# Attention units split into three steps in a fused attention and mixture kernel on one Trainium2 core

## Chip, core and metric

The kernel runs on one core of a Trainium2 chip. The metric is the device time of one execution in microseconds, as the median of several runs; lower is better. The profile is of one more execution of the same program. Its engines are PE (matrix products; its weight loads are shown as PEld), DVE, ACT and POOL (elementwise work), and SP, which issues the DMA transfers.

## What is computed

Three stages follow each other, all in float32.

```
scores = q @ k.T / sqrt(64), masked to 32 keys (heads 0-3) or 32 keys with stride 4 (heads 4-7)
x      = softmax(scores) @ v                      # 4 batches, 8 heads, 576 positions -> 2304 x 512
g      = sigmoid(x @ w_gate) * (x @ w_val)        # 512 -> 1536
x      = g @ w_out                                # 1536 -> 512
logits = x @ phi                                  # 2304 x 32 slots
slots  = softmax over tokens(logits).T @ x        # 32 x 512
slots  = relu(slots @ w1[e]) @ w2[e]              # 8 experts, 4 slots each
out    = softmax over slots(logits) @ slots
```

## The kernel before

The 2304 tokens are five blocks: blocks 0 to 3 have 512 tokens each, block 4 has 256. The attention of a block is four units, each a pair of heads. A unit goes through scores (a group of products of 32 by 64 at line 170 that fills two PSUM banks `s_ps`), a softmax (largest value at L184 and difference at L187 on DVE, exponential at L196 on ACT, sum and reciprocal at L201 to L203 on DVE, division at L207 on POOL), a turn of the probabilities (`turn_unit`, transposes at L219, a copy by ACT at L220 into `pt_ring`), the weighted sums of values (`weighted`, products of 64 by 32 at L246), and `finish_unit`, which takes the sums out of PSUM into the operand `x_hi`, `x_lo` of the next stage. The sums of unit z-2 are written into the free halves of the two banks that unit z's scores use.

The gated layer of a block is twelve tiles. A tile is two halves, a = 0 for the gate and a = 1 for the value; a half is twelve products of 128 by 512 at L494 into one of two PSUM banks `l1ps`. A tanh on ACT (L505) empties the first, a multiplication on DVE (L480) the second; the product of the next tile that uses the bank has to wait for it. The weights of a tile are split into a high and a low part (`whl`, L451 on ACT and L452 on DVE or POOL), in two buffers.

In the head (`first_block`) the four units of block 0 are worked off in an order written by hand, with the first products of tile 0 between them. There `fixed[0]` is true and the instructions keep the order of the program on each engine. After that a scheduler places them, but for the attention's instructions on PE and the loads, which stay in order among themselves. While the twelve tiles of block 0 run, their weights come from packed integers: a transfer into `st`, a top part by ACT (L380), a shift and a low part on DVE (L384, L387), two sums on POOL (L391), and a transfer back to memory. This is `convert`, and `ahead(z)` calls it for tile z. In the same loop the units of blocks 1 to 4 are interleaved: `attn_steps` makes a list of steps, and a `Spread` object, called once after each half, emits as many of them as its table of marks (count of halves, steps due) asks for.

The steps of before are two kinds. `sp_step(z)` has the scores of unit z, at once behind them the weighted sums of unit z-2, the softmax of z, the finish of z-2 and loads; `t_step(z-1)` turns unit z-1. While the tiles of block 1 run, six further conversions give the matrix w_out, and `slot_weights` has each go through four small steps, due some halves later by the list `later`: two turns (`wt_ps`, L428), one product with phi (`pt_ps`, L434), and one sum of products (`wp_ps`, L443). From there on the kernel has no attention: blocks 2 and 3 run their layer with a seven-product scheme (`pa`, `pd`, `pe` at L618), block 4 and the slots' sums follow, then the experts and the output.

Of the kernel before, what the change touches and what calls it, by code (L numbers as in the profile page):

```python
# [22 lines left out]
NF = 12  # L23
# [30 lines left out]
def tile_kernel(  # L54
# [154 lines left out]
    def softmax(u, norm):  # L209
        soft_max(u)  # L210
        soft_exp(u)
        soft_sum(u)
        soft_norm(u, norm)
# [87 lines left out]
    def attn_steps(pbs, norm):  # L301
        jobs = [(n, hp) for n in pbs for hp in HP_ORDER]
        us = [{"id": j, "z": z} for z, j in enumerate(jobs)]

        def load_qk(z):
            if z < len(us):
                start_unit(us[z], "qk")

        def load_v(z):
            if z < len(us):  # L310
                start_values(us, z)

        begun = []

        def first(what):
            if what not in begun:
                begun.append(what)
                what(0)
                what(1)

        def sp_step(z):
            if z < len(jobs):
                if z == 0:
                    first(load_qk)
                    first(load_v)
                scores(us[z], range(4))
                if 2 <= z:
                    weighted(us[z - 2], range(2), us[z])
                softmax(us[z], norm)
                load_qk(z + 2)  # L330
                if z == 0:
                    load_v(2)
            if z >= 2:
                if z >= len(jobs):
                    weighted(us[z - 2], range(2))
                finish_unit(us[z - 2])
                load_v(z + 1)

        def t_step(z):
            turn_unit(us[z])  # L340

        steps = []
        for z in range(len(jobs) + 2):
            steps += [(sp_step, z)] + ([(t_step, z - 1)] if 0 < z <= len(jobs) else [])
        return steps, lambda: first(load_qk), lambda: first(load_v)


# [63 lines left out]
    ticks = [0]  # L411
    later = []
# [7 lines left out]
    def slot_weights(f, wo_f, lag):  # L420

        wt = pm.rearrange("p a b -> p (a b)").rearrange("p (k c x) -> p k c x", k=ND, c=2)
        at_ = {}

        def turned(c):
            wt_ps = ps_a.tile([P, ND, P], F32, tag="a", name="wt_ps")
            for kc in range(ND):
                nc.tensor.transpose(wt_ps[:, kc], wo_f[:, c, P * kc : P * kc + P], ident)  # L428
            nc.scalar.copy(wt[:, :, c], wt_ps)

        def product():
            pt_ps = ps_m.tile([P, 2, P], F32, tag="m", name="pt_ps")
            for kc in range(ND):
                nc.tensor.matmul(  # L434
                    pt_ps[32 * kc : 32 * kc + 32], lhsT=phi[:, kc, :], rhs=wt[:, kc], start=True, stop=True
                )
            at_["pt"] = acc[:, 2, 0:256].rearrange("p (c x) -> p c x", c=2)
            nc.vector.tensor_copy(at_["pt"], pt_ps)

        def summed():  # L440
            wp_ps = ps_m.tile([P, 2, 32], F32, tag="m", name="wp_ps")
            for c in range(2):
                nc.tensor.matmul(wp_ps[:, c], lhsT=at_["pt"][:, c], rhs=i4, start=True, stop=True)  # L443
            nc.vector.tensor_scalar(wp[:, f : f + 2], wp_ps, 0.5, None, ALU.mult)

        for n, (step, *args) in enumerate(((turned, 0), (turned, 1), (product,), (summed,))):
            later.append((ticks[0] + lag + n, step, args))

    def split_half(whl, src, h, eng):
        src = src.rearrange("p (a k c) -> p a k c", a=2, k=ND)  # L450
# [6 lines left out]
    def split_w(src, pool=(True, False)):  # L457
        whl = new_w()
        for h in range(2):
            split_half(whl, src, h, nc.gpsimd if pool[h] else nc.vector)  # L460
        return whl
# [407 lines left out]
    conv = {}  # L869

    def ahead(z):
        if z < NF:
            conv[z] = convert(z)
# [21 lines left out]
    def first_block():  # L895
# [43 lines left out]
        whl = new_w()  # L939
# [7 lines left out]
        convert_end(0, fw[0])  # L947
        fw[1] = convert_begin(1)
        first_qk()
        first_v()  # L950
        g = l1_tile(0, 0)
        pt = [ps_l1.tile([P, 512], F32, tag="l1", name="l1ps") for _ in range(2)]

        def chunk(dc):
            for a in range(2):
                l1_chunk(0, whl, a, pt[a], dc)
# [11 lines left out]
        whl1 = new_w()  # L968
# [3 lines left out]
        split_half(whl1, fw[1][:, 1], 1, nc.vector)  # L972
        convert_end(1, fw[1])
        ahead(2)
        chunk(HP_ORDER[2])
        chunk(HP_ORDER[3])
        for a in range(2):
            l1_gate(g, a, pt[a])
        return whl1

    steps, first_qk, first_v = attn_steps([1, 2, 3, 4], nc.gpsimd)
    sab = Spread(steps, [(2, 0), (2 * NF - 2, 10), (4 * NF - 4, len(steps))])
    fixed[0] = True
    whl = first_block()
    fixed[0] = False
    ahead(3)
    sab.n = 2

    def load_w(z):
# [2 lines left out]
            ld(nc.sync.dma_start(wst[z], wg32[z]))  # L992

    for f in range(1, NF):
        whl = split_w(conv.pop(f), (False, False)) if f > 1 else whl
        ahead(f + LA + 1)
        if f >= 10:
            store()
            load_w(f - 10)
        l1(0, f, whl, sab)  # L1000
        if f == 3:
            pad_stream()
# [44 lines left out]
    for f in range(NF):  # L1047
        whl = split_w(wst[f // 2][:, f % 2])
# [436 lines left out]
```

## Time and profile before

| what | us |
|---|---|
| median of 3 runs | 482.8 |
| lowest, highest run | 481.75, 483.62 |
| the profiled execution | 484.0 |
| its span, first to last instruction | 482.2 |
| outside the span | 1.8 |
| PE busy, share of the span | 465.4, 97% |
| DVE, ACT, POOL busy | 302.9, 211.7, 159.0 |

A page of the profile gives the busy time of each engine, then groups of instructions by line. In a timeline each row has its start and its length in microseconds, the engine, the line, the operation, what is written and read, and how many equal ones follow each other. Square brackets at the end hold the idle time of the engine just ahead of the row and the line that released it; "issue" stands for a wait for nothing that the profile shows. The length of a matrix product contains the time in which it drains, while the next is under way already, so the pace of PE is the distance between starts and not the length.

### The profile page before, as it was taken

How to read it: one execution, taken by the hardware profiler on the slowest of the kernel's cores; microseconds unless marked ns; L12 is line 12 of the kernel's file. 1: busy time of each engine (PE TensorE's matmuls, PEld its weight loads, DVE VectorE, ACT ScalarE, POOL GpSimd, SP SyncE). 2: the span in 40 equal slices, each digit the busy share in tenths (PEclk: the TensorE clock that was granted, in tenths of full speed). 3: DMA queues.
4: the chain of work that ended last, by engine and by line, in shares of the span. 5: the costliest groups of instructions: out<-in, count | busy, mean ns of one | idle time of the engine just before them, and what ended most of it. 6: DMA issues, size and time to landing. Idle time of an engine off the chain costs nothing.

```text
span 482.2 us, 12644 instructions
## 1 busy us (share of the span) xinstructions
PE 465.4 (97%) x5424; PEld 357.8 (74%) x5424; DVE 302.9 (63%) x591; ACT 211.7 (44%) x395; POOL 159.0 (33%) x134
## 2 busy tenths in 40 slices
PE   7899999999989999999999999999999999999993
PEld 3577788887868787686788888888887889842552
DVE  5867899666567675467776566656547765532623
ACT  2645555435445544444355545554535344300222
POOL 1335566226444843612033332333312124110100
PEclk9999999999989999999999999999999999999998
DMA  8997999775995883022220220210599986589966
GB/s 327 416 390 255 395 331 370 258 266 193 344 386 215 271 307 121 37 90 87 90 87 1 88 88 1 87 54 34 176 374 419 349 335 236 217 330 368 427 242 239
DMA packets 23720, 112.12 MB, mean 233 GB/s; under 512 B 2288, under 2 KB 7152, under 8 KB 14576
## 3 DMA queue, kind: packets, MB, share of 16 engines
q1 hardware_dynamic: 23664, 111.32, 61.6%
q8 instruction: 42, 0.69, 0.5%
q14 instruction: 14, 0.11, 0.1%
HBM read 97.16 MB, written 14.16 MB: 231 GB/s over the span
## 4 chain that ended last, share of the span: by engine, by line
PE 87%; DVE 5%; POOL 2%; ACT 2%; issue 2%; DVEq 0%; POOLq 0%; ACTq 0%
PE l1ps L494 32%; PE pa L618 13%; PE pe L618 7%; PE tp L751 4%; PE so_ps L1314 3%; PE pd L618 3%; PE s_ps L246 3%; PE h_ps L1252 3%; PE s_ps L170 3%; PE sp L776 2%; PE lt_ps L722 2%; POOL fw L391 2%; PE wt_ps L428 1%; PE tr L219 1%; PE op L1352 1%
## 5 line engine op out<-in xcount | busy, mean ns | idle before, releaser
L494 PE MATMUL l1ps<-x_hi,whl 128*128 128x512 f32 x384 | 130.9, 405 | 0.9 <-ACT g L505 0.9
L494 PEld LDWEIGHTS l1ps<-x_hi,whl 128*128 128x128 f32 x384 | 72.8, 190 | 17.4 <-ACT g L505 1.8
L494 PE MATMUL l1ps<-x_lo,whl 128*128 128x512 f32 x192 | 75.8, 395 | 0.0
L391 POOL TENSOR_TENSOR fw<-fw 128x512 int32<-128x512 int32 x36 | 48.5, 1366 | 43.9 <-DVE fw L384 23.7
L494 PEld LDWEIGHTS l1ps<-x_lo,whl 128*128 128x128 f32 x192 | 36.6, 191 | 6.7 <-DVE x_lo L275 0.4
L480 DVE SCALAR_TENSOR_TENSOR g<-g,l1ps 128x512 f32<-128x512 f32 (+1 forms) x36 | 21.4, 595 | 27.0 <-PE l1ps L494 26.8
L494 PE MATMUL l1ps<-x,whl 128*128 128x256 f32 x288 | 37.0, 285 | 0.0
L494 PEld LDWEIGHTS l1ps<-x,whl 128*128 128x128 f32 x288 | 35.4, 192 | 0.4 <-ACT whl L451 0.2
L505 ACT ACTIVATE g<-l1ps 128x512 f32<-128x512 f32 (+1 forms) x36 | 18.9, 524 | 35.7 <-PE l1ps L494 35.5
L452 POOL TENSOR_TENSOR whl<-w,whl 128x512 fp32r<-128x512 f32 x12 | 15.9, 1326 | 51.3 <-ACT whl L451 39.7
L452 POOL TENSOR_TENSOR whl<-wst,whl 128x512 fp32r<-128x512 f32 x12 | 15.9, 1323 | 33.8 <-ACT whl L451 28.8
L452 DVE TENSOR_TENSOR whl<-fw,whl 128x512 fp32r<-128x512 f32 x24 | 23.7, 1001 | 5.2 <-ACT whl L451 4.7
L207 POOL TENSOR_TENSOR sm<-sm,su 128x512 f32<-128x512 f32 x14 | 18.9, 1353 | 22.0 <-DVE su L203 22.0
L751 PEld LDWEIGHTS tp<-cst,g 128*128 128x128 f32 x192 | 21.3, 140 | 5.4 <-issue 4.1
L751 PE MATMUL tp<-cst,g 128*128 128x128 f32 x192 | 25.0, 275 | 0.0
L756 ACT COPY gt<-tp 128x512 f32<-128x512 f32 x24 | 14.0, 584 | 24.1 <-PE tp L751 21.4
L184 DVE TENSOR_REDUCE mx<-s_ps 128x4 f32<-128x256 f32 x40 | 15.1, 415 | 14.4 <-PE s_ps L246 9.5
L681 DVE TENSOR_TENSOR tm<-pe,tm 128x512 f32<-128x512 f32 x12 | 8.3, 692 | 24.6 <-PE pe L618 24.6
L380 ACT ACTIVATE fw<-st 128x1024 f32<-128x1024 f32 x18 | 20.7, 1149 | 4.9 <-DMA st<-wd 4.9
L451 ACT CAST whl<-fw 128x512 fp32r<-128x512 f32 x24 | 14.6, 624 | 15.4 <-POOL fw L391 9.1
L451 ACT CAST whl<-wst 128x512 fp32r<-128x512 f32 x24 | 14.3, 618 | 15.1 <-PE l1ps L494 10.7
L246 PE MATMUL s_ps<-pt_ring,v 64*64 64x32 f32 (+1 forms) x992 | 17.9, 220 | 2.4 <-issue 1.6
(485 smaller groups left out, 958.1 us busy)
## 6 DMA issues: line engine op xcount, KB each, us to landing
ew<-w SPq DMA_DIRECT2D x32, 1024.0 KB, 7.8
st<-wd SPq DMA_DIRECT2D x18, 1024.0 KB, 8.7
wst<-wg SPq DMA_DIRECT2D x12, 1024.0 KB, 5.8
v<-qkv SPq DMA_DIRECT2D x20, 512.0 KB, 7.0
wg<-fw SPq DMA_DIRECT2D x12, 512.0 KB, 5.5
w<-wg SPq DMA_DIRECT2D x6, 1024.0 KB, 6.7
qk<-qkv SPq DMA_DIRECT2D x10, 576.0 KB, 6.0
qk<-qkv SPq DMA_DIRECT2D x8, 528.0 KB, 5.5
```

The source lines that it names most:

```text
L184: kp(nc.vector.tensor_reduce(mx[:, 4 * r : 4 * r + 4], u["s_ps"][r], AX.X, ALU.max))
L207: kp(norm.tensor_tensor(s, s, u["su"].unsqueeze(2).to_broadcast([P, 8, 64]), ALU.mult))
L246: nc.tensor.matmul(o, lhsT=v[k, t, i, r, :], rhs=p_[k, 2 * r + t, i, 0:nq], start=True, stop=True)
L380: return kp(nc.scalar.activation(fw[:, 0, c], staged[z][:, c, 1].bitcast(F32), AF.Prelu, scale=2.0**-112, alpha=2.0**32))
L391: kp(nc.gpsimd.tensor_tensor(low, top, low, ALU.add))
L451: kp(nc.scalar.copy(whl[:, 0, h], src[:, h]))
L452: kp(eng.tensor_tensor(whl[:, 1, h], src[:, h], whl[:, 0, h].bitcast(F32), ALU.subtract))
L480: return nc.vector.scalar_tensor_tensor(g, g, 1.0, val, ALU.add, ALU.mult)
L494: nc.tensor.matmul(pt, lhsT=whl[:, w_, a, dc, :], rhs=x_[n][:, dc, :], start=(dc == HP_ORDER[0] and (w_, x_) == (0, x_hi)), stop=(dc == HP ...
L505: return nc.scalar.activation(g, pt, AF.Tanh, scale=0.5) if a == 0 else gated(g, pt)
L618: nc.tensor.matmul(pt, lhsT=w[:, w_, P * c : P * c + P], rhs=x_[:, c], start=first and c == 0 and w_ == 0 and x_ is hi, stop=c == 1 and w_ ...
L751: nc.tensor.transpose(tp[:, c], g_sb[self.n, 4 * q + c][:, P * j : P * j + P], ident)
```

## The change

The step of a unit's scores (`s_step`) no longer holds the weighted sums of the unit two before. These, with their finish and the load of values, are a step of their own (`w_step`), placed behind the turn of the unit between. For the four units of block 4 the sums stay inside the step of the scores. The marks of `Spread` are new: from 10 steps at the end of block 0's tiles to 16 (of a list that has 44 steps and not 34), with a mark for the start. In the head the loads of values for the first units of block 1 are issued behind the conversion of tile 2, and the conversion of tile 3 and the split of tile 2's weights are called before the head's end, so that they keep the program's order. The last of the four small steps of `slot_weights` is due one half later (n + n // 3 gives 0, 1, 2, 4).

```
-        def sp_step(z):
-            if z < len(jobs):
-                if z == 0:
-                    first(load_qk)
-                    first(load_v)
-                scores(us[z], range(4))
-                if 2 <= z:
-                    weighted(us[z - 2], range(2), us[z])
-                softmax(us[z], norm)
-                load_qk(z + 2)
-                if z == 0:
-                    load_v(2)
-            if z >= 2:
-                if z >= len(jobs):
-                    weighted(us[z - 2], range(2))
-                finish_unit(us[z - 2])
-                load_v(z + 1)
+        def s_step(z):
+            if z == 0:
+                first(load_qk)
+                first(load_v)
+            scores(us[z], range(4))
+            if us[z]["id"][0] == 4:
+                w_step(z - 2)
+            softmax(us[z], norm)
+            load_qk(z + 2)
+            if z == 0:
+                load_v(2)
...
+        def w_step(z):
+            weighted(us[z], range(2), us[z + 2] if z + 2 < len(jobs) else None)
+            finish_unit(us[z])
+            load_v(z + 3)
...
         for z in range(len(jobs) + 2):
-            steps += [(sp_step, z)] + ([(t_step, z - 1)] if 0 < z <= len(jobs) else [])
+            if z < len(jobs):
+                steps.append((s_step, z))
+            if 0 < z <= len(jobs):
+                steps.append((t_step, z - 1))
+            if z >= 2 and (z >= len(jobs) or jobs[z][0] < 4):
+                steps.append((w_step, z - 2))
...
-            later.append((ticks[0] + lag + n, step, args))
+            later.append((ticks[0] + lag + n + n // 3, step, args))
...
         first_qk()
-        first_v()
         g = l1_tile(0, 0)
...
         ahead(2)
+        first_v()
         chunk(HP_ORDER[2])
         chunk(HP_ORDER[3])
         for a in range(2):
             l1_gate(g, a, pt[a])
-        return whl1
+        ahead(3)
+        return whl1, split_w(conv.pop(2), (False, False))
...
-    sab = Spread(steps, [(2, 0), (2 * NF - 2, 10), (4 * NF - 4, len(steps))])
+    sab = Spread(steps, [(2, 0), (5, 1.5), (2 * NF - 2, 16), (4 * NF - 4, len(steps))])
...
-    ahead(3)
...
-        whl = split_w(conv.pop(f), (False, False)) if f > 1 else whl
+        whl = split_w(conv.pop(f), (False, False)) if f > 2 else begun[f - 1]
```

From line 318 on the lines of the changed kernel stand up to four further down: L380 is L384 there, L451 is L455, L494 is L498, L505 is L509.

The first place is ACT at the end of the head, from the conversion of tile 2 on. Before:

```order
L380 ACTIVATE fw<-st 128x1024
L505 ACTIVATE g<-l1ps 128x512
L451 CAST whl<-fw 128x512 x2
L196 ACTIVATE sm_96<-sm_96 128x512
L380 ACTIVATE fw<-st 128x1024
L505 ACTIVATE g<-l1ps 128x512
```

And now:

```order
L384 ACTIVATE fw<-st 128x1024
L509 ACTIVATE g<-l1ps 128x512
L384 ACTIVATE fw<-st 128x1024
L509 ACTIVATE g<-l1ps 128x512
L455 CAST whl<-fw 128x512 x4
L196 ACTIVATE sm_96<-sm_96 128x512
```

The tanh of tile 1 (the second `g<-l1ps`) stood behind the exponential of block 1's first unit (L196) and tile 3's conversion (L380); it now stands ahead of the exponential.

The second place is PE in block 1's tiles, at the unit whose scores are in `s_ps_2016` and `s_ps_2017`; the rows of scores (L170) and of sums (L246) repeat, 32 of each, and the first of each bank stands for them. Before:

```order
L156 MATMUL s_ps_2017<-msk 128x256
L170 MATMUL s_ps_2016<-qk 32x64
L170 MATMUL s_ps_2017<-qk 32x64
...
L246 MATMUL s_ps_2016<-pt_ring,v_1682 64x32
L246 MATMUL s_ps_2017<-pt_ring,v_1682 64x32
...
L434 MATMUL pt_ps<-pm,cst 32x256 x4
L428 MATMUL wt_ps<-cst,fw 128x128 x4
```

And now:

```order
L156 MATMUL s_ps_2017<-msk 128x256
L170 MATMUL s_ps_2016<-qk 32x64
...
L438 MATMUL pt_ps<-pm,cst 32x256 x4
L432 MATMUL wt_ps<-cst,fw 128x128 x4
L498 MATMUL l1ps<-x_hi,whl 128x512
...
L219 MATMUL tr<-cst,sm_96 128x128 x4
L432 MATMUL wt_ps<-cst,fw 128x128 x4
L498 MATMUL l1ps<-x_hi,whl 128x512
...
L246 MATMUL s_ps_2016<-pt_ring,v_1702 64x32
```

The weighted sums that followed the scores at once now come behind two halves of a tile (two groups of twelve L498) and the turn of another unit.

The third place is POOL at the end of block 1's tiles, where `pt_ring<-pt_ring,su` is the division of a unit's softmax, the last such row being the last unit's. Before:

```order
L546 TENSOR_TENSOR tsum<-xf 128x512 x2
L452 TENSOR_TENSOR whl<-wst,whl 128x512
L207 TENSOR_TENSOR pt_ring<-pt_ring,su 128x512
L546 TENSOR_TENSOR tsum<-xf,tsum 128x512 x4
L452 TENSOR_TENSOR whl<-wst,whl 128x512 x2
```

And now:

```order
L207 TENSOR_TENSOR pt_ring<-pt_ring,su 128x512
L550 TENSOR_TENSOR tsum<-xf,tsum 128x512 x2
L456 TENSOR_TENSOR whl<-wst,whl 128x512
L207 TENSOR_TENSOR pt_ring<-pt_ring,su 128x512
L550 TENSOR_TENSOR tsum<-xf,tsum 128x512 x2
L456 TENSOR_TENSOR whl<-wst,whl 128x512
```

The last unit's division now stands behind one more split of weights, that of the last tile; the split before it (tile 10) is among rows further up.

## Rows read from the trace of the kernel before

**Rows 1.** The page: busy time by engine, instruction transfers, a group of lines.

```profile
PE 465.4 (97%) x5424; PEld 357.8 (74%) x5424; DVE 302.9 (63%) x591; ACT 211.7 (44%) x395; POOL 159.0 (33%) x134
q8 instruction: 42, 0.69, 0.5%
```

**Rows 2.** Stretches: length, then busy time (instructions) by engine, granted clock, DMA.

```profile
40.00:130.00 90.00, 90.00 (x1446) 72.67 (x1444) 68.65 (x121) 44.94 (x76) 46.15 (x34) 1.00 0.85 308
130.00:210.00 80.00, 77.82 (x1235) 61.53 (x1232) 51.59 (x107) 40.32 (x78) 39.50 (x31) 0.98 0.61 214
```

**Rows 3.** PE's waits: line, who released it, total, times, longest.

```profile
PE s_ps L246 <- issue: 1.6, 1, 1.6
...
PE wp_ps L443 <- DVE x L275: 0.6, 1, 0.6
```

**Rows 4.** Timeline, SP, ACT and PE at the end of the head.

```profile
20.91 0.91 SPq L299 DMA_DIRECT2D v<-qkv  x2
22.95 0.33 SPq L360 DMA_DIRECT2D st<-wd  x1
...
35.58 0.63 ACT L196 ACTIVATE sm<-sm 128x512 f32<-128x512 f32 x1 [2.08 <-DVE sm L187]
36.12 1.11 ACT L380 ACTIVATE fw<-st 128x1024 f32<-128x1024 f32 x1
...
36.48 0.39 PE L494 MATMUL l1ps<-x_hi,whl 128*128 128x512 f32 x1
...
37.12 0.59 ACT L505 ACTIVATE g<-l1ps 128x512 f32<-128x512 f32 x1
...
37.76 0.50 PE L494 MATMUL l1ps<-x_hi,whl 128*128 128x512 f32 x1 [0.89 <-ACT g L505]
```

**Rows 5.** Timeline, PE at the unit of 137 us.

```profile
137.24 0.86 PE L170 MATMUL s_ps<-qk 64*32 64x64 f32 x64
...
138.03 0.82 PE L246 MATMUL s_ps<-pt_ring,v 64*64 64x32 f32 x41
...
140.41 0.55 PE L246 MATMUL s_ps<-pt_ring,v 64*64 64x32 f32 x23 [1.56 <-issue]
```

**Rows 6.** The stretch behind it, columns as in rows 2.

```profile
140.00:146.00 6.00, 5.59 (x46) 4.37 (x47) 3.44 (x9) 1.90 (x4) 0.00 (x0) 0.72 1.02 419
```

**Rows 7.** Timeline, PE: sums that stand alone between two halves.

```profile
205.04 1.12 PE L246 MATMUL xp<-pt_ring,v 64*64 64x16 f32 x64
206.09 0.50 PE L494 MATMUL l1ps<-x_hi,whl 128*128 128x512 f32 x1
206.43 0.39 PE L494 MATMUL l1ps<-x_lo,whl 128*128 128x512 f32 x1
206.66 0.62 PE L494 MATMUL l1ps<-x_hi,whl 128*128 128x512 f32 x2
```

**Rows 8.** Timeline, PE, ACT and POOL from the last unit's scores to its turn.

```profile
186.99 0.39 PE L156 MATMUL s_ps<-msk 128*128 128x256 bf16 x2
...
189.16 0.63 PE L443 MATMUL wp_ps<-cst,acc 128*128 128x32 f32 x4
189.62 0.64 PE L428 MATMUL wt_ps<-cst,fw 128*128 128x128 f32 x4
...
192.88 0.60 PE L219 MATMUL tr<-cst,pt_ring 128*128 128x128 f32 x4
193.19 1.04 POOL L207 TENSOR_TENSOR pt_ring<-pt_ring,su 128x512 f32<-128x512 f32 x1 [3.97 <-DVE su L203]
...
193.97 0.50 PE L494 MATMUL l1ps<-x_hi,whl 128*128 128x512 f32 x1
...
196.92 0.67 PE L246 MATMUL xp<-pt_ring,v 64*64 64x32 f32 x32
197.07 1.14 ACT L451 CAST whl<-wst 128x512 fp32r<-128x512 f32 x2 [2.92 <-POOL tsum L546]
...
199.17 1.73 POOL L452 TENSOR_TENSOR whl<-wst,whl 128x512 fp32r<-128x512 f32 x1
```

More of the change, by code (lines that the diff above doesn't have):

```diff
@@ L978, in first_block @@
             l1_gate(g, a, pt[a])
-        return whl1
+        ahead(3)
+        return whl1, split_w(conv.pop(2), (False, False))
     steps, first_qk, first_v = attn_steps([1, 2, 3, 4], nc.gpsimd)
-    sab = Spread(steps, [(2, 0), (2 * NF - 2, 10), (4 * NF - 4, len(steps))])
+    sab = Spread(steps, [(2, 0), (5, 1.5), (2 * NF - 2, 16), (4 * NF - 4, len(steps))])
     fixed[0] = True
-    whl = first_block()
+    begun = first_block()
     fixed[0] = False
-    ahead(3)
     sab.n = 2
```

## The prediction

> **What bounds the kernel now.** I read the busy table first: PE is busy for 465.4 of 482.2 us, 97% [rows 1], and the next engine for 302.9. So PE's own order decides, and a change can only give back time in which PE stands still or runs slowly, or cost such time. Then the stretches in which the change works: from 40 to 130 us PE has no gap at all, and from 130 to 210 us it is busy for 77.82 of 80 us at a granted clock of 0.98 [rows 2]. Then PE's waits, of which three lie in the part that is reordered: 1.6 us inside the weighted sums with no releaser that the profile shows, 0.6 us for DVE ahead of a sum of products [rows 3], and 0.89 us for a tanh at the end of the head [rows 4]. Behind 210 us the instructions of PE stand in the same order as before, so what lies there only shifts.
>
> All that can be won is therefore small: these three waits, and what the clock loses behind the first of them.
>
> **The change part by part.** The sum is made against the profiled execution, 484.0 us (a span of 482.2 and 1.8 around it). It is 1.2 us above the median of 482.8, so it may hold more of a stall that comes and goes than a usual run does.
>
> *The head.* PE's product of tile 2 waits from the end of the half that starts its last product at 36.48 until 37.76 [rows 4]. Products follow each other at 0.23 us (206.43 to 206.66 in [rows 7]), so 1.28 - 0.23 = 1.05 us are lost. It waits for the tanh that starts at 37.12, and that stood on ACT behind the exponential (35.58, held for 2.08 us by DVE) and tile 3's conversion (36.12). In the new order of ACT the tanh stands ahead of the exponential, and only the conversion precedes it. That needs its transfer: the load of `st` is issued at 22.95, once its buffer is free, with two loads of values just ahead of it (20.91) that now stand behind. Its data can only come earlier. Even a conversion that starts as late as 33 us, with 1.11 us, lets the tanh end at about 34.7, well ahead of 36.7. So 1.05 us go. The two loads of values are first read by the first weighted sums of block 1, which stand behind the scores of two more units, so I cost their delay at nothing; the split of tile 2's weights, now in fixed order, also keeps its place ahead of PE, though with little to spare. Bounds: 1.05 won, or nothing.
>
> *Scores and sums apart.* At 138 us PE gets through 41 of 64 products of the sums, stands still for 1.56 us and goes on [rows 5]; nothing that the profile shows releases it. The scores have 64 products and 64 weight loads, the sums as many. The page has 42 instruction transfers of 0.69 MB together, against 5424 products and 5424 loads on PE [rows 1]: 10848 / 42 = 258 instructions for each. On the mean such a load lasts 482.2 / 42 = 11.5 us, but scores and sums in one piece use one up in 2.17 us (186.99 to 189.16 in [rows 8]). I therefore take the stall for a lack of instructions, in a piece that uses them five times as fast as the mean. The change breaks these pieces: of 14 units whose scores are followed at once by sums, the four of block 4 remain, and one place has sums and then scores. At the place of the stall two halves of a tile lie between. I count the 1.56 us as gone. Behind the stall the clock is granted at 0.72 over 6 us [rows 6], which is time at 1.2 GHz and not 2.4; PE has just stood still and then only had small products. It cost 6 x 0.28 = 1.7 us, which goes too. Together 3.3 us; bounds 0 and 3.3.
>
> The Trainium skill (Runtime: NRT & Kernel Launch, section Instruction fetch mechanics) says that the sequencer fetches the next block while it executes the current one, so that crossing a block is mostly hidden. By that rule the stall is none of instructions, breaking the pieces wins nothing, and the sum is higher by 3.3 us; that is the second rival below. The row with its 1.56 us and no releaser speaks against it here, without settling it.
>
> *More breaks.* Every group of small products between two halves has its price: the first product behind it takes 0.34 us to the next start (206.09 to 206.43) where others take 0.23 [rows 7]. Sums alone take 1.05 us (205.04 to 206.09), about what they add behind scores, so the group itself costs nothing more. In the new order of PE 42 groups stand between halves where 36 stood, so 6 x 0.11 = 0.7 us are added. Bounds: 0.3 and 1.2.
>
> *Later sums of products.* The wait of 0.62 us for DVE at 200 us [rows 3] came from a sum of products that needed a PSUM buffer of the last units' sums. Half a tile later the buffer should be free: 0.6 us won, at worst nothing. The other five such sums had no wait, so their delay brings nothing.
>
> *The last unit's turn.* Here a wait is added. The last unit's scores come one half later than before, with one half and eight products left until its turn. From their start to the turn PE has scores and sums 2.17 us, the turn of another unit and a product with phi 1.09 (192.88 to 193.97), a sum of products 0.46 (189.16 to 189.62), a half of 2.95 (193.97 to 196.92) and eight products of 0.23 with one break, 1.95: in all 8.6 us [rows 8]. The division that this turn needs now stands on POOL behind a split of tile 11's weights, and the cast that the split needs starts when the half has ended (197.07 against 196.92), which is 2.17 + 0.46 + 1.09 + 2.95 = 6.7 us from the scores. Then one cast of two in 1.14 us, 0.57; POOL's split of 1.73; the division of 1.04: 10.0 us. PE waits about 1.4 us, and what is queued behind the turn on PE, four products and the last sums, waits with it. Bounds: 0, if the scheduler's order gives way, and 2.0, if POOL waits for both casts.
>
> *Banks.* A unit's two banks are now held until its later sums, half a tile longer, and the transposes `wt_ps` share the four banks. Each unit still ends its use ahead of the next but one's scores, so I take nothing.
>
> The sum: 484.0 - 1.05 - 3.3 - 0.6 + 0.7 + 1.4 = 481.15, so 481.1 us. Against the median of 482.8 that is 0.35% less, inside the 0.5% (2.4 us) that a measurement of this kernel can tell from no change; faster begins below 480.4, slower above 485.2.
>
> **The rivals.** *The last turn does not wait.* If the division is done in time, 1.4 us are saved: 479.7 us, faster. For it: POOL stood idle for 3.97 us ahead of the same division before [rows 8]. Against it: the order of POOL.
>
> *The change does not remove the stall.* If what holds PE at 138 us is not the density of instructions, the stall and its clock come back somewhere in the run: 481.1 + 3.3 = 484.4 us, no change. For it: the other thirteen dense pieces had no such wait; against it: this one lies in the middle of one, at a time when DMA, which brings the instructions too, is busy throughout (1.02 in [rows 6]).
>
> *The clock falls in a longer lump.* In two places at the end of block 1, turn, scores, sums, sum of products, product with phi and transposes now stand in one row, 2.17 + 1.09 + 0.46 = 3.7 us and the transposes, without a product of a tile [rows 8]. If the clock goes down behind one as in [rows 6], 1.7 us: 482.8 us, no change.
>
> *The tanh falls behind in block 0's tiles.* This one ends slower. In the new order of ACT a tanh still stands behind an exponential at four later tiles, and exponentials wait for DVE, whose queue now gets a unit's scores earlier and more of them before tile 12 (16 steps against 10). Where the exponential, a conversion and the tanh start only when the bank is wanted, PE waits 0.63 + 1.11 + 0.59 = 2.3 us [rows 4]; at half of that in four places 4.6 us: 485.7 us. It decides from the point where the exponential starts later than a half's 12 x 0.23 = 2.75 us behind its tanh's product. Against it: from 40 to 130 us PE had no gap at all with similar queues [rows 2].
>
> **How the numbers follow.** Forecast, 481.1 us: 0.45, of which 0.06 lie below 480.4. Last turn without a wait, 479.7: 0.22. Stall remains, 484.4: 0.15. Clock in a lump, 482.8: 0.06. Tanh behind, 485.7: 0.12. Faster by over 0.5%: 0.22 + 0.06 = 0.28. Slower: 0.12. Within: 0.60. The range goes from 479.3, the first rival with the low end of the breaks, to 484.6, just over the stall that remains; it leaves out the slower rival and a little below, some 0.18. Most of the chance lies on one side of zero or within, so it needs no second range.
>
> **What would show it.** Right: no wait of PE at the end of the head; none inside scores or sums, and a clock of 1.00 from 130 to 210 us; one wait of 1 to 2 us of the last turn for POOL near 200 us; PE's first product of block 0's logits 2 to 4 us earlier. Wrong: an idle time "issue" inside sums again; waits of products for the tanh between 50 and 110 us; a stretch at half clock; waits of the scores for a bank or a load.

## The result, and the profile after

The changed kernel takes 485.83 us in the median of 13 runs (483.51 to 488.75), the kernel before 482.8 (13 runs, 481.12 to 484.29); the ratio is 1.0065, with a 95% interval of 1.004 to 1.0091. It is 0.65% slower, and 485.83 lies outside the range of 479.3 to 484.6. The prediction was wrong. All ratios compare fast runs; of the experiment f3 the profiled execution (491.94 us) was a slow one, and only the places and lengths of single stalls are read from it.

The page of the profiled execution (488.5 us), two lines that answer to [rows 1], and the stretches of [rows 2], with the two in which the clock fell (length, busy time and instructions by engine, granted clock, DMA share, GB/s):

```profile
PE 469.4 (96%) x5424; PEld 358.0 (74%) x5424; DVE 305.3 (63%) x591; ACT 212.0 (44%) x395; POOL 158.6 (33%) x134
q8 instruction: 42, 0.69, 0.5%
```

```profile
40.00:130.00 90.00, 89.79 (x1381) 71.03 (x1380) 67.92 (x126) 43.78 (x75) 42.10 (x32) 1.00 0.81 289
130.00:210.00 80.00, 76.56 (x1245) 60.18 (x1244) 51.45 (x103) 39.54 (x76) 41.67 (x33) 0.98 0.61 223
170.00:178.00 8.00, 7.09 (x119) 5.63 (x102) 3.53 (x12) 1.49 (x3) 2.89 (x4) 0.79 0.49 117
...
425.00:435.00 10.00, 9.94 (x63) 4.78 (x62) 3.42 (x8) 0.93 (x3) 0.98 (x1) 0.83 0.72 275
```

From 130 to 210 us PE is busy for 1.3 us less than before, so it stands still more, and the clock still falls there, 30 us later than in [rows 6]. PE's waits, against [rows 3]:

```profile
PE tr L219 <- POOL pt_ring L207: 1.8, 1, 1.8
PE s_ps L246 <- issue: 1.6, 2, 0.9
...
PE l1ps L498 <- ACT g L509: 0.2, 1, 0.2
```

The wait of `wp_ps` for DVE is gone, and that for the tanh at the end of the head (the 0.2 us that are left for a tanh lie at 58.7 us and cost 0.3 from start to start): on ACT the conversion stands ahead and the tanh behind it starts 4 us earlier than in [rows 4].

```profile
30.86 1.14 ACT L384 ACTIVATE fw<-st 128x1024 f32<-128x1024 f32 x1 [0.87 <-DMA st<-wd]
33.09 0.60 ACT L509 ACTIVATE g<-l1ps 128x512 f32<-128x512 f32 x1 [1.10 <-PE l1ps L498]
```

The idle time "issue" inside the sums has the same total of 1.6 us, now in two places. The wait of the last turn for POOL is new. PE's timeline (start, time busy, idle before) at the two stalls, against [rows 5]:

```profile
163.33 0.90 PE L246 MATMUL s_ps<-pt_ring,v 64*64 64x32 f32 x46
164.92 0.53 PE L246 MATMUL s_ps<-pt_ring,v 64*64 64x32 f32 x18 [0.69 <-issue]
...
170.19 0.55 PE L246 MATMUL s_ps<-pt_ring,v 64*64 64x32 f32 x22
171.65 0.83 PE L246 MATMUL s_ps<-pt_ring,v 64*64 64x32 f32 x42 [0.91 <-issue]
```

Both units are of block 4, the ones whose sums the change leaves behind their scores. From start to start the two stalls cost 0.91 and 1.13 us, the one of before 1.78. What follows at half clock costs 8 x 0.21 = 1.7 us, as in [rows 6], and a spell between 425 and 435 us another 1.7, where the order of PE is that of before.

The turn of the last unit, on PE, DVE and POOL, against [rows 8]:

```profile
198.53 0.69 DVE L484 SCALAR_TENSOR_TENSOR g<-g,l1ps 128x512 f32<-128x512 f32 x1 [0.80 <-PE l1ps L498]
199.14 0.20 DVE L203 RECIPROCAL su<-su 128x8 f32<-128x8 f32 x1
```

```profile
199.36 1.28 POOL L456 TENSOR_TENSOR whl<-wst,whl 128x512 fp32r<-128x512 f32 x1 [5.12 <-ACT whl L455]
200.60 1.49 POOL L207 TENSOR_TENSOR pt_ring<-pt_ring,su 128x512 f32<-128x512 f32 x1
```

```profile
199.92 0.39 PE L498 MATMUL l1ps<-x_lo,whl 128*128 128x512 f32 x1
202.15 0.66 PE L219 MATMUL tr<-cst,pt_ring 128*128 128x128 f32 x4 [1.83 <-POOL pt_ring L207]
```

The wait is there for the reason given: POOL's split stands ahead of the division. On DVE the gate of a half, which cannot start before that half ends, also stands ahead of the reciprocal (198.53 ahead of 199.14), but it does not count here: the reciprocal is done at 199.34, and POOL is busy with the split until 200.6. Start to start the wait costs 2.23 - 0.23 = 2.0 us. From the start of the unit's scores (191.69) PE comes to the turn in 8.5 us, and POOL is done with the division after 10.4: the cast ahead of the split starts 0.3 us later than in the forecast, and the split 0.1 us later behind it.

The breaks, a half that ends in scores (first four rows) and one that ends in sums standing alone, against [rows 7]:

```profile
61.36 0.39 PE L498 MATMUL l1ps<-x_hi,whl 128*128 128x512 f32 x1
61.59 0.39 PE L156 MATMUL s_ps<-msk 128*128 128x256 bf16 x2
...
62.70 0.50 PE L498 MATMUL l1ps<-x_hi,whl 128*128 128x512 f32 x1
63.03 0.40 PE L498 MATMUL l1ps<-x_lo,whl 128*128 128x512 f32 x1
...
68.54 0.39 PE L498 MATMUL l1ps<-x_hi,whl 128*128 128x512 f32 x1
68.85 1.14 PE L246 MATMUL s_ps<-pt_ring,v 64*64 64x32 f32 x64
69.92 0.50 PE L498 MATMUL l1ps<-x_hi,whl 128*128 128x512 f32 x1
70.26 0.39 PE L498 MATMUL l1ps<-x_lo,whl 128*128 128x512 f32 x1
```

Into the scores a product takes its usual 0.23 us (61.36 to 61.59), into the sums 0.31 (68.54 to 68.85); out of either 0.33 to 0.34. So sums alone add 70.26 - 68.54 - 2 x 0.23 = 1.26 us to the tile where sums behind scores add 1.06 (the experiment h4 below shows such a piece): 0.20 more. Ten units have their sums apart now, 2.0 us. The whole stretch agrees: from the first product of tile 2 to the first product of the logits, with waits and half clock taken out, PE needs 167.1 us before and 169.0 after.

The profiled executions then add up: head -1.05, `wp_ps` -0.8, stalls +0.26 (2.04 for 1.78), clock behind them 0, breaks +2.0, last turn +2.0, the tanh at 58.7 us +0.3, the spell at 425 us +1.7: +4.4 of the 4.5 us between 484.0 and 488.5.

### The profile page after: what moved, and what is told of

It reads as the page before. It is cut to its first block, busy times and chain, and to the rows that moved or that the text cites. A ratio compares the mean times of both kernels' runs of the same rounds, so it can differ in the third digit from the quotient of the medians.

```text
span 486.7 us, 12643 instructions
## 1 busy us (share of the span) xinstructions
PE 469.4 (96%) x5424; PEld 358.0 (74%) x5424; DVE 305.3 (63%) x591; ACT 212.0 (44%) x395; POOL 158.6 (33%) x134
## 4 chain that ended last, share of the span: by engine, by line
PE 89%; DVE 6%; issue 2%; ACT 1%; POOL 1%; ACTq 0%; DVEq 0%; POOLq 0%
PE l1ps L498 31%; PE pa L622 13%; PE pe L622 6%; PE tp L755 4%; PE s_ps L246 3%; PE so_ps L1318 3%; PE pd L622 3%; PE h_ps L1256 3%; PE s_ps L170 3%; PE sp L780 2%; PE lt_ps L726 2%; PE tr L219 2%; DVE whl L456 2%; PE wt_ps L432 1%; PE idle L116 1%
## 5 line engine op out<-in xcount | busy, mean ns | idle before, releaser
L498 PE MATMUL l1ps<-x_hi,whl 128*128 128x512 f32 x384 | 131.9, 406 | 0.2 <-ACT g L509 0.2
L498 PEld LDWEIGHTS l1ps<-x_hi,whl 128*128 128x128 f32 x384 | 72.6, 190 | 16.9 <-ACT g L509 0.7
L498 PE MATMUL l1ps<-x_lo,whl 128*128 128x512 f32 x192 | 75.8, 395 | 0.0
L395 POOL TENSOR_TENSOR fw<-fw 128x512 int32<-128x512 int32 x36 | 49.7, 1402 | 43.9 <-DVE fw L388 30.0
L498 PEld LDWEIGHTS l1ps<-x_lo,whl 128*128 128x128 f32 x192 | 36.5, 190 | 6.5 <-DVE x_lo L275 0.4
L498 PE MATMUL l1ps<-x,whl 128*128 128x256 f32 x288 | 37.0, 285 | 0.0
L498 PEld LDWEIGHTS l1ps<-x,whl 128*128 128x128 f32 x288 | 35.4, 192 | 0.4 <-ACT whl L455 0.2
L509 ACT ACTIVATE g<-l1ps 128x512 f32<-128x512 f32 (+1 forms) x36 | 18.9, 524 | 27.4 <-PE l1ps L498 27.2
L207 POOL TENSOR_TENSOR sm<-sm,su 128x512 f32<-128x512 f32 x14 | 16.3, 1162 | 35.1 <-DVE su L203 34.7
L456 DVE TENSOR_TENSOR whl<-fw,whl 128x512 fp32r<-128x512 f32 x24 | 22.7, 964 | 3.9 <-ACT whl L455 3.5
L196 ACT ACTIVATE sm<-sm 128x512 f32<-128x512 f32 x16 | 10.1, 632 | 29.2 <-DVE sm L187 29.2
L384 ACT ACTIVATE fw<-st 128x1024 f32<-128x1024 f32 x18 | 20.7, 1152 | 4.3 <-DMA st<-wd 4.3
L455 ACT CAST whl<-wst 128x512 fp32r<-128x512 f32 x24 | 14.0, 622 | 19.1 <-PE l1ps L498 11.4
L455 ACT CAST whl<-fw 128x512 fp32r<-128x512 f32 x24 | 14.5, 621 | 16.5 <-POOL fw L395 9.9
```

The costliest lines, as they stand in the source:

```text
L207: kp(norm.tensor_tensor(s, s, u["su"].unsqueeze(2).to_broadcast([P, 8, 64]), ALU.mult))
L384: return kp(nc.scalar.activation(fw[:, 0, c], staged[z][:, c, 1].bitcast(F32), AF.Prelu, scale=2.0**-112, alpha=2.0**32))
L395: kp(nc.gpsimd.tensor_tensor(low, top, low, ALU.add))
L455: kp(nc.scalar.copy(whl[:, 0, h], src[:, h]))
L456: kp(eng.tensor_tensor(whl[:, 1, h], src[:, h], whl[:, 0, h].bitcast(F32), ALU.subtract))
L498: nc.tensor.matmul(pt, lhsT=whl[:, w_, a, dc, :], rhs=x_[n][:, dc, :], start=(dc == HP_ORDER[0] and (w_, x_) == (0, x_hi)), stop=(dc == HP ...
```

## The experiments

### What each part does

First each part alone on the kernel before. *e1_head*: the head's hunks of the change.

```
-        first_v()                        # from ahead of l1_tile
+        first_v()                        # to behind ahead(2)
...
+        ahead(3)
+        return whl1, split_w(conv.pop(2), (False, False))
```

> The kernel before with the change in the head alone (tile 3's conversion and tile 2's split ordered in the head, the loads of values later); the order of PE stays. If the head is worth what the trace of after shows there (the wait of the last product of tile 2 gone, 1.05 us), the time is 1.0 us under before (ratio 0.9978) and the chip's profile shows no wait of an l1ps product for a tanh near 37 us. The rival, that the time won is lost again in a stall of instructions further on, since everything behind runs an us earlier against the loads: 0 to +2 us, with an idle time called issue in scores or sums.

481.31 us against 481.45; ratio 0.9995 (0.9969 to 1.0022). The wait of the head is gone from the trace, and the stall stays where it was. The interval holds both -1.05 us (0.9978) and nothing: the time alone does not show the gain.

*e2_steps*: `s_step`, `t_step`, `w_step` and the new spread.

```
-        def sp_step(z):
+        def s_step(z): ...   def w_step(z): ...
-    sab = Spread(steps, [(2, 0), (2 * NF - 2, 10), (4 * NF - 4, len(steps))])
+    sab = Spread(steps, [(2, 0), (5, 1.5), (2 * NF - 2, 16), (4 * NF - 4, len(steps))])
```

> The kernel before with the steps apart and their new spread alone (head and sums of products as before). From the two traces: breaks of the rows of products cost 2.2 us more than before, the last unit's turn waits 1.8 to 2.0 us for POOL, and a stall of instructions with its clock costs as much as it did before or less. Theory one, the steps are the whole loss: 482.8 + 2.2 + 2.0 = 487.0 us (ratio 1.0085), or 484 us where the stall is gone too. Rival, the loss comes from the three parts together (buffers shared by the later sums of products): within 1 us of before.

487.51 us; ratio 1.0105 (1.0065 to 1.0145): the loss is in the steps, by its middle value more than in the whole change, though the two intervals overlap. Besides the breaks and the wait of the last turn (1.8 us again), a turn at 52 us waits, since without the head's new order the softmax of block 1's first unit comes late:

```profile
51.86 0.39 PE L498 MATMUL l1ps<-x_hi,whl 128*128 128x512 f32 x1
53.98 0.66 PE L219 MATMUL tr<-cst,sm 128*128 128x128 f32 x4 [1.73 <-POOL sm L207]
```

So the new spread needs the new head. And the wait of `wp_ps` for DVE is gone here without the later sums of products.

*e3_later*:

```
-            later.append((ticks[0] + lag + n, step, args))
+            later.append((ticks[0] + lag + n + n // 3, step, args))
```

> The kernel before with the sums of products half a tile later alone. If the wait of wp_ps for DVE (0.6 us near 200 us) goes and nothing else moves: 482.2 us, ratio 0.9988. Rival: the wait is taken over by the next user of the bank, ratio 1.000, with a wait of PE of 0.5 us or more for DVE or ACT near 200 us.

484.27 us; ratio 1.0051 (1.0024 to 1.0077), slower, which neither theory had. The wait of `wp_ps` goes, but 40 us earlier the later sum now stands just ahead of a product with phi, and the copy of `wp_ps` (162.45 on DVE) stands behind a conversion's shift and a step of a softmax (161.31, 1.23 us). The product starts 0.15 us after the copy is done (162.66); the brackets name the reciprocal that ends just behind it, at 162.77, when PE's wait is already over:

```profile
161.02 0.63 PE L428 MATMUL wt_ps<-cst,fw 128*128 128x128 f32 x4
...
162.45 0.21 DVE L444 TENSOR_SCALAR wp<-wp_ps 128x64 f32<-128x64 f32 x1
...
162.81 0.64 PE L434 MATMUL pt_ps<-pm,cst 128*32 128x256 f32 x8 [1.16 <-DVE su L203]
```

And a second stall in sums appears at 167.9 us (0.92 us), at 36 of 64.

*e4_head_later*: both edits.

> The kernel before with the head and the later sums of products, without the steps apart. If the parts add up: -1.05 - 0.6 = -1.65 us, 481.1 us, ratio 0.9966, the fastest of all so far. If the stall in the sums at 138 us depends only on where the blocks of instructions end, which these two edits leave as it was there, it stays at 1 to 1.6 us; if it depends on what the DMA does at the time, it may go or come elsewhere, 1.5 to 3.3 us to either side.

483.01 us; ratio 1.0024 (0.9992 to 1.0055). The same two stalls (0.73 and 0.89) and the same wait of the product for DVE, 1.2: what the head gives, the later sums take.

### The last turn and the breaks

*f1_last_dve*, on the changed kernel:

```
-            softmax(us[z], norm)
+            softmax(us[z], norm if z + 1 < len(jobs) else nc.vector)
```

> The changed kernel with the last unit's division on DVE instead of POOL, nothing else. If the wait of 1.8 us ahead of the last turn is the division behind the weight split on POOL, it goes and the time is 1.8 to 2.0 us under that of the changed kernel: 483.9 us or a ratio of 1.0025 to before. Rival: DVE's own queue (the gate of the half, the splits) holds the division as long, or what it displaces on DVE (a low part of weights) makes the next half wait: a wait of 1 us or more ahead of the turn or of an l1ps product stays, ratio 1.005 or more.

483.57 us against 482.55; ratio 1.001 (0.9988 to 1.0033), 0.55% under the changed kernel's. The wait shrinks, but does not go:

```profile
196.31 0.39 PE L498 MATMUL l1ps<-x_lo,whl 128*128 128x512 f32 x1
197.73 0.63 PE L219 MATMUL tr<-cst,pt_ring 128*128 128x128 f32 x4 [1.03 <-DVE pt_ring L207]
```

Without POOL's split 0.8 us are won. Now the gate ahead of the reciprocal does count, since the division follows it on the same engine, and the division takes 1.82 us on DVE (195.75). The profiled execution also had only one stall, of 0.40 us, so not all of the 0.55% need be the last turn's.

*f2_sums_behind*, on the changed kernel:

```
-            if us[z]["id"][0] == 4:
+            if z >= 2:
                 w_step(z - 2)
...
-                steps.append((w_step, z - 2))
+                steps.append((w_step, z - 2) if z >= len(jobs) else (none,))
```

> The changed kernel with every unit's sums directly behind the scores of the next but one again, as in block 4; the spread, the head and the later sums of products stay as changed. 38 rows of products of a tile instead of 43, and no sums that stand alone but the last. If a break costs 0.11 us, as the prediction had it, 0.55 us come back; if going from a product of a tile into the sums costs 0.21 us, where going into scores costs 0.13, and a turn ahead of sums 0.53 instead of 0.35, as the trace of after shows, 1.5 to 2.2 us come back. Against both: more pieces of 130 products and loads, so a stall of instructions of 1 us or more may show in one that had none.

486.03 us; ratio 1.0073 (1.0039 to 1.0107), no gain in time. In the trace the stretch from the first product of tile 2 to the first product of the logits, with waits and half clock taken out, is 167.1 us instead of 169.0 in the changed kernel: 1.9 us less, which is what 0.2 us for each unit's sums gives, and not 0.55. In this execution a stall of 2.7 us at 138 us, back in the piece that is whole again, its spell of half clock and a turn's wait of 0.9 us stand against the gain.

### What the stall is

PE's instructions can be counted in the trace: products, weight loads and the few that wait for a semaphore. In thirteen profiled executions of ten kernels 20 stalls of over 0.2 us lie inside sums between 40 and 215 us. Every one comes when the count is 193 or 194 past a multiple of 256 (by products and loads alone it would be 162 to 177), and every one ends 1.25 to 1.51 us after an instruction transfer has landed. The Trainium skill (Runtime: NRT & Kernel Launch, Instruction fetch mechanics) has instructions refilled in blocks of 256, which agrees. A block below is what one such transfer brings.

*f3_after_pad0* and *g1_head_pad4* shift the counts: eight or four fewer padding products, each of which stands in the trace as two products and two loads.

```
-PAD = 8
+PAD = 0        # on the changed kernel
...
-PAD = 8
+PAD = 4        # on the kernel before with the changed head
```

> The changed kernel without the 8 padding products of 128x8 that stand near 51 us (they cost 0.24 us together). Every instruction of PE behind them moves 32 places against the ends of the blocks in which instructions are loaded. If the stalls at 164 and 170.5 us are late blocks, asked for at 157.6 and 163.8 us while all DMA engines are full, they go, since the block ends then fall near 146, 155 and 166 us and not ahead of a dense piece; with them their clock, 2.0 + 1.7 us: 482 us, ratio 0.999. Rival: the stalls belong to these pieces themselves (a bank, a value that the profile does not name): they stay where they are and the time falls by 0.24 us alone, ratio 1.006.

> The kernel before with the changed head, and 4 padding products instead of 8 (0.12 us less; every instruction of PE behind 51 us moves 16 places against the block ends). If the stall of 1.5 us in the sums at 137 us is a late block, it goes (the block ends fall near 124, 135 and 147 us) and the time is 1.05 + 1.5 + 0.12 us under before, with the clock up to 1.7 more: 478.8 us, ratio 0.9944 or lower. Rival: the stall stays at its place, or comes back in a piece where a block end now falls: ratio 0.997 to 1.000.

485.15 us, ratio 1.0059 (1.0034 to 1.0083), and 482.54 us, ratio 0.9997 (0.9969 to 1.0024): the stalls did not go. But they moved inside their pieces, of f3:

```profile
167.65 1.13 PE L246 MATMUL s_ps<-pt_ring,v 64*64 64x32 f32 x62
169.13 0.30 PE L246 MATMUL s_ps<-pt_ring,v 64*64 64x32 f32 x2 [0.35 <-issue]
...
174.16 0.78 PE L246 MATMUL s_ps<-pt_ring,v 64*64 64x32 f32 x38
177.05 0.59 PE L246 MATMUL s_ps<-pt_ring,v 64*64 64x32 f32 x26 [2.11 <-issue]
```

and of g1:

```profile
139.23 0.90 PE L246 MATMUL s_ps<-pt_ring,v 64*64 64x32 f32 x48
141.76 0.43 PE L246 MATMUL s_ps<-pt_ring,v 64*64 64x32 f32 x16 [1.63 <-issue]
```

46 and 22 products became 62 and 38, by 16, which is what eight padding products stand for; 40 (in e1) became 48, by 8. So a stall belongs to a count of instructions and not to a bank or a value. The shift of 32 and 16 places that I had worked out held, my claim that the block ends would then miss the pieces did not: scores and sums in one piece are 130 products and as many loads, 260 instructions, and a block end always falls into such a piece or just behind it. Shifting does not take it out of such a piece; breaking the piece or freeing the DMA might. These are the next two.

*h1_one_apart*, on the kernel before: the sums of one unit half a tile later, behind the turn.

```
-                if 2 <= z:
+                if 2 <= z and z not in (10,):
                     weighted(us[z - 2], range(2), us[z])
...
             turn_unit(us[z])
+            if z + 1 in (10,):
+                weighted(us[z - 1], range(2), us[z + 1])
+                finish_unit(us[z - 1])
+                load_v(z + 2)
```

> The kernel before with one piece broken and nothing else: the sums that stood behind the eleventh unit's scores (where PE stood still at 138 us) come half a tile later, behind the turn. In all kernels so far the stall comes at the same count of PE's instructions, 193 or 194 past a multiple of 256; that place now lies 28 places earlier in the sums, and PE gets there 2.9 us later. If the block of instructions lands at its own time (it landed at 139.0), PE finds it there: 1.6 us and the 1.4 to 1.7 us of clock behind it go, a turn ahead of sums costs 0.2 more: ratio 0.994 to 0.998. Rival: another block, near 168 us, takes over (its slack before was the smallest of the rest): ratio 0.998 to 1.001.

*h4_less_load*, on the kernel before: a quarter of each load of the output layer's weights, read four times, so that the kernel computes something else with PE's order as it was.

```
+        cols = 2048 if z < NF else 512
-        ld(nc.sync.dma_start(staged[z].rearrange("p a b -> p (a b)"), wd[z].bitcast(U32)))
+        ld(nc.sync.dma_start(staged[z].rearrange("p a b -> p (a b)")[:, 0:cols], wd[z].bitcast(U32)[:, 0:cols]))
```

> The kernel before with a quarter of each of the six loads of the output layer's weights left out to a quarter (0.25 instead of 1 MB each, the conversion reads that quarter four times; so the output is not the reference's). PE's order is that of before. If the block for 138 us is late because the DMA engines are full from 118 to 147 us, it lands earlier by the 2 us and more that 0.75 MB less in each burst take, and the stall in the sums is gone with its clock: 1.6 to 3.3 us less in that stretch. Rival: the block is late because it is asked for only 1.9 us behind the one before it, whatever the loads do: it starts 7 to 8 us behind its crossing still, and the stall stays at 1.0 us or more.

Neither has a stall in any sums from 40 to 215 us. The sums of the same unit, whole, with their neighbours, in h1 and in h4:

```profile
141.57 0.60 PE L219 MATMUL tr<-cst,sm 128*128 128x128 f32 x4
142.10 1.14 PE L246 MATMUL s_ps<-pt_ring,v 64*64 64x32 f32 x64
```

```profile
137.54 1.14 PE L246 MATMUL s_ps<-pt_ring,v 64*64 64x32 f32 x64
138.60 0.64 PE L443 MATMUL pt_ps<-pm,cst 128*32 128x256 f32 x8
```

When the block landed is in the DMA queues (packets, MB, share of the engines' time): before from 131.7 to 138 us,

```profile
q1 hardware_dynamic: 421, 2.09, 98.0%
```

with no instruction transfer at all; from 138 to 139.1, and in h4 already from 131.9 to 133:

```profile
q1 hardware_dynamic: 100, 0.45, 101.6%
q8 instruction: 1, 0.02, 5.5%
```

```profile
q1 hardware_dynamic: 68, 0.27, 91.7%
q8 instruction: 1, 0.02, 5.5%
```

With the same order of PE, which comes to the end of the block before at 133.07 us in before and at 132.59 in h4, 0.75 MB less in each load bring the block 6 us earlier (its forerunner 3.6). In two more executions of before, k1 and k2 below, it lands at 139.2 and 137.8 us, so the 132.9 of h4 is no chance. It is late because it shares full DMA engines with the loads; the rival, that it is asked for too soon behind its forerunner, falls. When a block is asked for, the trace does not show. In h1 it lands as late as before (by 138.3 us), and PE needs it 4 us later. The times are 481.77 against 482.33 us for h1, ratio 0.9992 (0.9968 to 1.0016), and 481.56 for h4, 0.9983 (0.9967 to 0.9999): less than the trace of before had promised.

*k1_before_again*, *k2_before_again*, *k3_after_again* and *k4_one_apart_again* (no edit to before, before, after and h1) ask why, one profiled execution each.

> The kernel before, unchanged, a second profiled execution. If the stall belongs to the place, PE stands still in the sums near 138 us again, at the same count of products (41 of 64), for 0.7 to 1.8 us; if the clock's spell hangs on the stall's length, it follows a stall over 1.5 us and not one of 0.7.

> The same a third time: stall at 41 of 64 again. If a spell of half clock that is missing at 140 us comes at 425 us instead, the stretch from the first logits product to the end takes 1.7 us more in such an execution (274.8 instead of 273.1 us).

> The changed kernel, unchanged, a second profiled execution. If the loss is in the order of PE, the last turn waits 1.8 to 2.0 us for POOL again and the rows of products cost as much; the stalls near 164 and 170 us come at the same counts (46 and 22 of 64) with another length. Rival: those stalls are a matter of that one execution: none, and the time is 2 to 4 us lower than 488.5.

> The kernel with the one piece apart, a second profiled execution: no stall in any sums from 40 to 215 us. If the spell at 425 us replaces the one at 140 us, it is there again (274.8 us from the first logits product to the end); if it was chance, 273.1 us and a time near 480.5 us.

483.41, 481.16, 486.23 and 481.40 us. Of k1, k2 and k3:

```profile
139.38 0.82 PE L246 MATMUL s_ps<-pt_ring,v 64*64 64x32 f32 x41
140.54 0.55 PE L246 MATMUL s_ps<-pt_ring,v 64*64 64x32 f32 x23 [0.33 <-issue]
```

```profile
137.66 0.82 PE L246 MATMUL s_ps<-pt_ring,v 64*64 64x32 f32 x41
139.23 0.55 PE L246 MATMUL s_ps<-pt_ring,v 64*64 64x32 f32 x23 [0.74 <-issue]
```

```profile
165.96 0.53 PE L246 MATMUL s_ps<-pt_ring,v 64*64 64x32 f32 x18 [0.41 <-issue]
...
172.41 0.83 PE L246 MATMUL s_ps<-pt_ring,v 64*64 64x32 f32 x42 [0.67 <-issue]
```

The stall of before is at 41 of 64 each time, but of 0.55 and 0.96 us from start to start instead of 1.78, and without half clock behind it. Those of after are at 46 and 22 again, 0.63 and 0.89, the clock stays at 1.00, and the wait of the last turn is 1.8 us as before. So the place is fixed and the length changes from one execution to the next; the first profile of before held a long stall and a spell of half clock, together 2.5 to 2.9 us above these two (k1 still took 483.41 us, since its head ended 1.4 us later). k4 has no stall and no spell at 425 us, so the one that h1 had there (273.2 us from the first product of the logits to the end, 274.8 in h1) did not take the place of another.

### The parts that pay

*h2_head_one_last*: the head, the one unit apart, and the last of the six sums of products later.

```
+            later.append((ticks[0] + lag + n + (n // 3 if f == 10 else 0), step, args))
```

> As the one before, with the changed head (1.05 us) and the last of the six sums of products half a tile later (0.8 us), without the other breaks of the change. If all three add up: -1.05 - 0.8 - 1.4 to -3.1 us, ratio 0.990 to 0.993, the fastest of all. Rival: everything behind the head runs an us earlier against the same loads, so a late block near 168 us costs 1 to 2.5 us again: 0.995 to 0.998.

480.73 us against 482.33; ratio 0.9973 (0.9951 to 0.9995). None of the waits of [rows 3] and [rows 4] is left, and no stall from 40 us on. It is the fastest of all, by 0.27% (1.3 us) against before and by some 0.9% against the changed kernel (0.9973 / 1.0065), but not by the 0.7 to 1% expected. The two waits alone give 1.85 us in the trace, so the stall's share cannot be told from nothing here; with h1 and h4 it is 0 to 1 us, not 3.3.

*h3_head_two_last* puts a second unit's sums later (`(10, 13)` in place of `(10,)`).

> As the one before, with the sums behind the fourteenth unit's scores (near 168 us) half a tile later too, where the next block end falls into a piece while the loads run. If a late block shows there in the kernel with one piece broken, this one is 1 to 2.5 us faster than that one; if not, it is 0.2 us slower, by one more turn ahead of sums.

486.28 us; ratio 1.0081 (1.005 to 1.0111). It tells nothing of late blocks: unit 13 is of block 4, whose softmax lies in the ring of turned probabilities, so the later sums read what it has overwritten, and wait 2.9 us for POOL's division: this kernel computes something else.

## Why the prediction was wrong, point by point

- *The head*, -1.05: right in the trace of every kernel that has it. ACT came as forecast, the tanh behind one conversion and ahead of the exponential. By time alone it is not proved (e1: -1.5 to +1.1 us).
- *Scores and sums apart*, -3.3: the step that failed most. Cause and place were right (a late block of instructions; the stall at 138 us goes when its piece is broken: h1). Two sizes were wrong. The prediction took the one execution's 1.56 us and its 1.7 us of clock as what every run pays; k1 and k2 show 0.55 and 0.96 and no clock. And "the four of block 4 remain" was written down and then costed at nothing: with other pieces and other times the late blocks fall into two of these, 0.63 to 1.13 us each. The term is about +0.75 instead of -3.3 against a usual execution (1.52 in k3, 0.75 in the mean of k1 and k2).
- *More breaks*, 0.7 (0.3 to 1.2): mis-sized, 2.0. It counted groups, six more, and took the price of the way out (0.11) alone. The way into sums costs 0.08 more than into scores, and it is the ten units with sums apart, not the six more groups, that count: 0.20 each. [Rows 7] held the way out; the row ahead of them, with the way in, was not read.
- *Later sums of products*, -0.6: the wait went, 0.8 from start to start, but e2 shows that the steps alone remove it, and e3 that the edit by itself costs a wait of 1.2 us elsewhere. "The other five had no wait, so their delay brings nothing" left out that a delay can make one.
- *The last unit's turn*, +1.4 (0 to 2.0): the mechanism was right, the size 2.0, at the upper bound. PE was 0.1 us faster than the count of 8.6 us, and POOL's division ended after 10.4 us and not 10.0. It did not wait for both casts, which is what the bound was made of.
- *The rivals*: the last turn does wait; no stretch of turn, scores and sums by itself brought the clock down in k3 (its lump of 3.7 us stood at 1.00); the tanh behind exponentials did not come, PE waits 0.2 us for it in all. The stall that remains came true in a worse form. Slower came from a mechanism that was in the sum with the wrong price, not from the slower rival.

By the sum with the measured sizes, against a usual execution: -1.05 + 0.75 - 0.8 + 2.0 + 2.0 = +2.9 us; the medians differ by 3.0. Two of the signs of being wrong came, an idle time "issue" inside sums and a stretch at half clock. Of the signs of being right, the last shows the loss in one row: PE's first product of the logits was to come 2 to 4 us earlier, and starts at 211.90 us instead of 209.04.

## What to carry to other kernels

Before a group of small instructions is taken out of a neighbour's company, price its way in and its way out from a row where it stands alone, and count the groups that change their neighbour, not the groups that are added. A wait with no releaser in a dense row of small products is worth a count of instructions: if it comes at the same count modulo a block in several executions, look at what else the DMA engines carry then, and break that one piece rather than all. Read a stall's length from more than one execution before it becomes the largest term of a sum.

## What the runs showed of the hardware that was not expected

A late block of PE's instructions ends its stall 1.25 to 1.51 us after its transfer has landed, in all 20 cases. A transfer of 16 KB was 6 us later because of data loads (98% of the engines' time taken), while most of the 42 blocks cost nothing. The Trainium skill (the same section) calls the crossing mostly hidden; that agrees with most of the 42 here, and two of the others cost 0.6 to 1.1 us each in after and k3.

The same count stops PE in the head too, which the account above leaves out. In all 18 traces PE stands still ahead of a turn at 18 to 21 us, at 193 or 194 past a multiple of 256 and 1.2 to 1.5 us after a transfer of instructions; the idle time goes from 0.1 us (e1) to 2.0 (e4), and from 0.7 to 1.4 among the three executions of before. Of after:

```profile
19.32 0.66 PE L219 MATMUL tr<-cst,sm 128*128 128x128 f32 x4 [1.36 <-issue]
```

So a part of what sets one execution apart from the next lies there.

Half clock (1.2 for 2.4 GHz, some 3.4 us, 1.7 us lost) followed stalls of 1.78, 1.85, 2.33 and 2.70 us, and two of 0.91 and 1.13 within 7 us; it did not follow stalls of 0.55 to 0.96, one of 1.53, nor the same pair at 0.63 and 0.89. In the head it followed the four longest idle times (1.7 to 2.0 us, in e4, f3, h2 and h3) and none of the others (up to 1.4). That looks like a matter of length, but the last turn's wait of 1.8 us was followed by half clock in e2 and not in after, f2 and k3. What decides is open, and so is the spell between 420 and 435 us, which five of the fifteen traces of changed kernels hold with PE's order unchanged there.
